# The two halves of a matmul's moving operand read in turn: both products of a dense layer, the spectral mix and the last transform step

## The chip, the cores and the metric

The kernel runs on one core of one Trainium2 chip. The metric is the device time of one launch in microseconds (us), lower is better. Times of before and after are medians over several runs; the profile is one execution, recorded instruction by instruction. PE is TensorE's matmul, PEld its weight load, DVE is VectorE, ACT is ScalarE, SP is SyncE.

## The reference, cut to what matters

A spectral layer is followed by a dense layer with squared ReLU, on 8 sequences of 3008 tokens with 256 features, all float32.

```python
X = np.fft.rfft(x, axis=1)
Yr = Xr @ w_r - Xi @ w_i + b_r
Yi = Xr @ w_i + Xi @ w_r + b_i
Yr = np.sign(Yr) * np.maximum(np.abs(Yr) - 0.01, 0.0)   # Yi likewise
y = np.fft.irfft(Yr + 1j * Yi, n=3008, axis=1)
h = np.maximum(y.reshape(24064, 256) @ w_in, 0.0)       # w_in: 256 x 2048
out = h * h @ w_out                                     # w_out: 2048 x 256
```

## The kernel before, in words

The transform of length 3008 is split in two factors, 47 and 64, and both directions are matmuls with small tables. Stage A is the step over 47, stage B the step over 64, then comes the mix (the product with `w_r` and `w_i`), a threshold, stage C (the inverse step over 64) and stage D (the inverse step over 47). Stages A and C leave their results in DRAM scratch, from which the next stage loads them. The dense layer follows, in 47 chunks of `CH` = 512 tokens; `HALF` is 256.

Most products are made in three matmuls on operands of type float32r: each float32 operand is split in a high and a low part, and `mm3` (lines 183 to 188) issues high x high (L186), high x low (L187) and low x high (L188) into one accumulator. Its first pair of arguments is the stationary operand, of up to 128 columns, which a weight load puts into the array before every matmul; its second pair is the moving operand, whose columns stream through the array and come out in the same order. Stages B and D use plain float32 matmuls (L228, L277), and so does the start's stage A (L488).

After a start of some 130 us, which works on the first two sequences, the kernel runs in rounds. A chunk has `NU` = 8 rounds, and there are 376 rounds and 3 more to finish. Round r does the following on TensorE, in this order:

1. `mm1`: the first product for two blocks of 128 hidden features, 12 matmuls with 512 moving columns each, from the chunk's operand `xt` (tile of 128 x 2 x 512, high and low). In 130 rounds the last of the 12 is made in two halves of 256 columns (L986).
2. at the place called "p1", and again at "p2" behind `mm2`: at each at most one piece of another stage, put there by a planner. Such a piece is stage A (6 matmuls), stage B (8), the mix (18 matmuls of 256 moving columns, with `wm` as the moving operand), stage C (3 of 512 columns, with `zh` and `zl` moving) or stage D (8).
3. `mm2`: the second product for the round three before (`LAG` = 3). It is a fast scheme with 7 block products in place of 8, on 7 combinations `g` of hidden blocks and token halves: 14 matmuls with `gh` (L1023) and 7 with `gl` (L1027), all of 256 moving columns. The last round of all has its own order in `mm2_last` (L1008).

ACT takes `ph` out of PSUM (L995), squares it (L996) and casts the 7 combinations to their high part (L1132); DVE makes the combinations (L1001 to L1003) and the low part (L1137). Behind these stand ACT's and DVE's work for the other stages, among it the copy of stage C's result from PSUM to the tile `evc` (L860), which is stored to scratch. `put_together` (L1030 and after) sums the 7 products of a chunk, and two transfers store it.

The order on every engine is written out by hand: the program issues round after round, place after place, and each engine works strictly in that order. The moving operands are read in rows that lie together: `xt` 512 elements of 4 bytes, `gh`, `gl` and `wm` 256, and `zh`, `zl` 512 over two neighbouring parts `q`.

`tables_main` runs once, at the end of the start, and writes the mix's weights `wm`: the high part by ACT (L180), the low part by DVE (L181), 128 x 768 elements in each of 2 steps. The start's own mix uses the same tile in another layout before that. Also in the start, `narrow` has ACT read every second 4-byte word of a tile of float64 weights (L301), beside casts of the same size that read words in a row (L431).

Of the kernel before, what the change touches and what calls it, by code (L numbers as in the profile page):

```python
# [9 lines left out]
F32 = mybir.dt.float32  # L10
# [6 lines left out]
S = 3008  # L17
# [4 lines left out]
D = 256  # L22
# [112 lines left out]
NU = NF // 2  # L135


CH = 512
HALF = CH // 2


def pair_rounds(nb):
# [9 lines left out]
def fft_mix_moe(ctx: ExitStack, tc: tile.TileContext, xp, xu, w_ri, b_ri,  # L152
                w_in, w_out, t_u, t_a, t_b, t_b0, t_m, t_d, sgn, outT):
    nc = tc.nc
# [6 lines left out]
    def ctile(name, shape, dt=F32):  # L161
        return const.tile(shape, dt, name=name, tag=name)
# [10 lines left out]
    wm = [ctile(f"wm{k}", [P, 3, 2, D], F32R) for k in range(2)]  # L173
    ctile("gap5", [P, 16])
    wi_ = []
    wo_ = [], []

    def split(src, hi, lo, engine=nc.vector):

        nc.scalar.copy(hi, src)  # L180
        engine.tensor_sub(lo, src, hi.bitcast(F32))  # L181
# [18 lines left out]
    def scratch2(b):  # L200
        scr2[b] = dr.tile([NR, N2, 2 * D], F32, tag="s2", name=f"s2_{b}")
# [4 lines left out]
    def load_b(b, i, t):  # L206
        v = scr1[b].rearrange("r n (c d) -> (n c) r d", c=2)
        nc.sync.dma_start(out=t.rearrange("p (q d) -> p q d", q=2), in_=v[:, 2 * i:2 * i + 2, :])
# [22 lines left out]
    def take_b(x, ps):  # L231
        nc.scalar.copy(x[:, 0:2].rearrange("p s k m -> p k s m"),  # L232
                       ps.rearrange("p (k s m) -> p k s m", k=2, s=2))

    def sum_x(x):
        nc.vector.tensor_add(x[:, 2], x[:, 0], x[:, 1])
# [22 lines left out]
    xts = {}  # L259
# [51 lines left out]
    def start():  # L311

        with ExitStack() as own:
# [4 lines left out]
            def tl(tag, shape=(P, 512), dt=F32, bufs=1, name=None):  # L318
                return sb.tile(list(shape), dt, tag=tag, name=name or tag, bufs=bufs)
# [36 lines left out]
            ms = tl("wmf", (P, 6, D))  # L356
# [39 lines left out]
            def tables_main():  # L396

                for k in range(2):
                    split(ms[:, 3 * k:3 * k + 3], wm[0][:, :, k], wm[1][:, :, k])
                    yield  # L400
                split(tM, tMs[:, 0], tMs[:, 1])
                yield
# [102 lines left out]
            xs, pm, zs, pc, got = {}, {}, {}, {}, {}  # L505
# [204 lines left out]
    def tl(tag, shape=(P, 512), dt=F32, bufs=1, name=None):  # L710
        return sb.tile(list(shape), dt, tag=tag, name=name or tag, bufs=bufs)

    def pst(name):
        return ps_f.tile([P, 512], F32, tag="f", name=name)

    def opnd(name, dt, bufs):
        return tl(name, (P, NPR, HALF), dt, bufs=bufs)

    for tag, shape, dt, bufs in (("g", (P, NPR, HALF), F32, 3), ("gh", (P, NPR, HALF), F32R, 2), ("gl", (P, NPR, HALF), F32R, 2),
                                 ("gap1", (P, 16), F32, 1), ("xh", (P, 3, 2, P), F32R, 1), ("xl", (P, 3, 2, P), F32R, 1),  # L720
# [74 lines left out]
    def plan_b(b, i, r):  # L795
        s = {}

        def load():
            if i == 0:
                scratch2(b)  # L800
            s["t"] = tl("ld", bufs=3, name="bin")
            load_b(b, i, s["t"])

        def points():
            s["ps"] = pst("psb")
            points_b(s["ps"], i, s["t"])

        def take():
            s["x"] = tl("x", (P, 3, 2, P), name="x")
            take_b(s["x"], s["ps"])  # L810

        def high():
            s["h"] = tl("xh", (P, 3, 2, P), F32R)
            nc.scalar.copy(s["h"], s["x"])

        def low():
            s["l"] = tl("xl", (P, 3, 2, P), F32R)
            nc.vector.tensor_sub(s["l"], s["x"], s["h"].bitcast(F32))

        def mix():  # L820
            p = s["p"] = pst("psm1"), pst("psm2")
            for comp, mat, bank, half in MIX:
                for k in range(2):
                    mm3(p[bank][:, half * D:half * D + D], (s["h"][:, comp, k], s["l"][:, comp, k]),
                        (wm[0][:, mat, k], wm[1][:, mat, k]), k == 0, k == 1)

        def biased():
            s["et"] = tl("et", (P, 2, 512))
            add_e(s["et"][:, 0], *s["p"])

        def threshold():
            e, t = s["et"][:, 0], s["et"][:, 1]
            nc.vector.tensor_scalar(t, e, LAM, -LAM, op0=ALU.min, op1=ALU.max)
            nc.vector.tensor_sub(e, e, t)

        def turned():
            z = s["z"] = tl("z", (P, 2, D))
            e = s["et"][:, 0].rearrange("p (c e) -> p c e", c=2)
            for q in range(2):
                r = 2 * i + q  # L840
                src = slice(64 * q, 64 * q + 64)
                nc.scalar.copy(z[:64, q], e[src, 0])
                nc.scalar.activation(z[64:, q], e[src, 1], AF.Copy, scale=sg[src, 1, r:r + 1])

        def zhigh():
            s["zh"] = tl("zh", (P, 2, D), F32R)
            nc.scalar.copy(s["zh"], s["z"])

        def zlow():
            s["zl"] = tl("zl", (P, 2, D), F32R)  # L850
            nc.vector.tensor_sub(s["zl"], s["z"], s["zh"].bitcast(F32))

        def back():
            s["ps"] = pst("psc")
            mm3(s["ps"], (tMs[:, 0], tMs[:, 1]),
                tuple(s[k].rearrange("p q e -> p (q e)") for k in ("zh", "zl")), True, True)

        def out():
            e = tl("ev", bufs=2, name="evc")
            nc.scalar.copy(e, s["ps"])  # L860
            store_c(b, i, e)

        at(r - 1, "load", load)
        at(r, "p1", points)
        at(r, "e", take)
        at(r, "e2", lambda: sum_x(s["x"]))
        at(r, "f", high)
        at(r, "v", low)
        at(r + 2, "p2", mix)
        at(r + 2, "f2", biased)  # L870
        at(r + 2, "v", threshold)
        at(r + 3, "a", turned)
        at(r + 4, "a", zhigh)
        at(r + 4, "v", zlow)
        at(r + BACK[b], "p2", back)
        at(r + BACK[b], "f", out)
# [79 lines left out]
    for c in range(1, nch):  # L956
# [5 lines left out]
        for n, part in enumerate(parts):  # L962
            at_b = flat[part[0]][0]
            lo = max(NU * (c - 1), free, rounds[at_b][-1] + BACK[at_b] + 3 if at_b else 2)
            got = spread(len(part), lo, NU * c - 3 - sum(map(len, parts[n + 1:])), D_WORK, 1, BESIDE)
# [5 lines left out]
    def mm1(c, j, halved):  # L971
        if c == 0 and 0 < j < LAG:
            ph = [ps_o.tile([P, CH], F32, tag=f"o{2 * j - 2 + a}", name="ph") for a in range(2)]
        else:
            t = ps_h.tile([P, 2, CH], F32, tag="h", name="ph")
            ph = [t[:, a] for a in range(2)]
        for a in range(2):
            f = 2 * j + a
            fs = slice(f * P, f * P + P)
            for k in range(2):  # L980
                w, x = (wi_[0][:, k, fs], wi_[1][:, k, fs]), (xts[c][0][:, k], xts[c][1][:, k])
                if halved and a and k:
                    nc.tensor.matmul(ph[a], w[0], x[0], start=False, stop=False)  # L983
                    nc.tensor.matmul(ph[a], w[0], x[1], start=False, stop=False)  # L984
                    for n in range(0, CH, HALF):
                        nc.tensor.matmul(ph[a][:, n:n + HALF], w[1], x[0][:, n:n + HALF], start=False, stop=n > 0)  # L986
                else:
                    mm3(ph[a], w, x, k == 0, k == 1)
        return ph
# [15 lines left out]
    def mm2_last(po, gh, gl):  # L1005

        def add(s, bank, half, w, x, stop):
            nc.tensor.matmul(po[bank][:, half * HALF:half * HALF + HALF], w[:, s], x[:, s],  # L1008
                             start=False, stop=stop, skip_group_check=True)

        for n in range(NPR + 2):
            if n < NPR:
                for k in range(2):
                    add(*LAST[n], wo_[k][NU - 1], gh, False)
            if n >= 2:
                add(*LAST[n - 2], wo_[0][NU - 1], gl, True)

    def mm2(j, po, gh, gl):

        for s, bank, half in PLACES:  # L1020
            out = po[bank][:, half * HALF:half * HALF + HALF]
            for k in range(2):
                nc.tensor.matmul(out, wo_[k][j][:, s], gh[:, s], start=j == 0 and half == 0 and k == 0,  # L1023
                                 stop=False, skip_group_check=True)
        for s, bank, half in PLACES:
            out = po[bank][:, half * HALF:half * HALF + HALF]
            nc.tensor.matmul(out, wo_[0][j][:, s], gl[:, s], start=False, stop=j == NU - 1,  # L1027
                             skip_group_check=True)

    def put_together(c, po):  # L1030
# [83 lines left out]
    with tc.manual_schedule():  # L1114
        for r in range(last + LAG):
            c, j = divmod(r, NU)
# [3 lines left out]
            if r < last:  # L1120
                ph = mm1(c, j, (r, "p1") not in plan)
# [3 lines left out]
            k = r - LAG  # L1125
# [86 lines left out]
```

## Time and profile before

| What | Value |
|---|---|
| time, median of 3 runs | 2524.14 us (2523.18 to 2525.43) |
| span of the profiled execution | 2521.5 us |
| TensorE busy with matmuls | 2503.5 us, 99% |
| TensorE busy with weight loads | 2260.2 us, 90% |
| DVE busy | 2097.8 us, 83% |
| ACT busy | 1991.8 us, 79% |
| granted TensorE clock | 1.000, mean of the span |

The span runs from the first to the last instruction of one execution. The page gives no separate time of that execution from outside; the runs' median stands 2.6 us above the span. Matmuls are pipelined, so the busy time of one (0.39 us for 512 columns) is longer than its share of the engine; the distance from one start to the next is that share.

### The profile page before, as it was taken

Reading aid. Unit: us, or ns where it says so; the run is one execution under the profiler, and the core shown is the slowest. Engines: PE = TensorE matmul, PEld = TensorE weight load, DVE = VectorE, ACT = ScalarE, POOL = GpSimd, SP = SyncE. Lnnn points to the kernel's source line nnn. Section 1 sums busy time; section 2 is a strip of 40 time slices with the busy share of each in tenths; the row PEclk is TensorE's granted clock in tenths of the full one; section 3 lists DMA queues with packets and bytes.
Section 4 is the critical chain, followed back from the end, with each engine's and each line's share of the span. In section 5 each row is a group of like instructions: output and inputs, shape, how many; then the busy total and the mean of one; then the engine's idle time right before and its main releaser. Section 6 shows DMA issues by size and latency. Waiting matters only on the chain.

```text
span 2521.5 us, 42247 instructions
## 1 busy us (share of the span) xinstructions
PE 2503.5 (99%) x16648; PEld 2260.2 (90%) x16648; DVE 2097.8 (83%) x3179; ACT 1991.8 (79%) x2776; POOL 17.0 (1%) x29
## 2 busy tenths in 40 slices
PE   9999999999999999999999999999999999999999
PEld 5689999999999999999999999999999999999998
DVE  5798888888888888888888888888887888777776
ACT  4788887888788887888878878788787788777776
POOL 0100000000000000000000000000000000000000
PEclk9999999999999999999999999999999999999999
DMA  8612222222121121212122121221111111101000
GB/s 266 207 55 66 74 88 68 65 76 73 54 75 60 50 70 57 71 50 67 60 69 63 54 70 50 70 62 61 58 56 56 38 54 48 39 21 34 17 25 18
DMA packets 110622, 164.66 MB, mean 65 GB/s; under 512 B 9513, under 2 KB 59673, under 8 KB 110234
## 3 DMA queue, kind: packets, MB, share of 16 engines
q1 hardware_dynamic: 110282, 161.85, 20.9%
q8 instruction: 132, 2.16, 0.4%
q14 instruction: 64, 0.52, 0.1%
q10 hardware_dynamic: 144, 0.13, 0.0%
HBM read 86.97 MB, written 74.97 MB: 64 GB/s over the span
## 4 chain that ended last, share of the span: by engine, by line
PE 88%; ACT 5%; DVE 4%; issue 1%; DMA 1%; SPq 0%; DVEq 0%; ACTq 0%
PE po L1023 21%; PE ph L187 11%; PE ph L188 11%; PE ph L186 11%; PE po L1027 11%; PE psd L277 3%; PE psb L228 3%; PE psm L186 3%; PE psm L188 3%; PE psm L187 3%; ACT g L995 1%; PE ph L986 1%; PE ph L983 1%; PE ph L984 1%; ACT g L996 1%
## 5 line engine op out<-in xcount | busy, mean ns | idle before, releaser
L1137 DVE TENSOR_TENSOR gl<-g,gh 128x1792 fp32r<-128x1792 f32 x376 | 759.5, 2020 | 22.4 <-ACT gh L1132 15.4
L995 ACT ACTIVATE g<-ph 128x512 f32<-128x512 f32 x752 | 408.2, 595 | 417.1 <-PE ph L188 297.4
L1023 PE MATMUL po<-gh,wo 128*128 128x256 f32 x5250 | 681.5, 280 | 3.1 <-DVE o L1053 2.1
L1132 ACT CAST gh<-g 128x1792 fp32r<-128x1792 f32 x376 | 637.2, 1695 | 3.5 <-PE po L1023 0.8
L1023 PEld LDWEIGHTS po<-gh,wo 128*128 128x128 f32 x5250 | 631.2, 188 | 6.5 <-DVE o L1053 5.9
L186 PE MATMUL ph<-xt,wi 128*128 128x512 f32 x1374 | 538.2, 392 | 2.2 <-ACT g L995 2.0
L188 PE MATMUL ph<-xt,wi 128*128 128x512 f32 x1374 | 537.4, 391 | 0.0
L187 PE MATMUL ph<-xt,wi 128*128 128x512 f32 x1374 | 537.3, 391 | 0.0
L1001 DVE TENSOR_TENSOR g<-g 128x512 f32<-128x512 f32 x376 | 259.3, 690 | 290.3 <-ACT g L996 288.4
L996 ACT ACTIVATE g<-g 128x1024 f32<-128x1024 f32 x376 | 399.5, 1062 | 12.0
L1027 PE MATMUL po<-gl,wo 128*128 128x256 f32 x2625 | 359.2, 276 | 0.0
L1027 PEld LDWEIGHTS po<-gl,wo 128*128 128x128 f32 x2625 | 325.7, 188 | 0.0
L188 PEld LDWEIGHTS ph<-xt,wi 128*128 128x128 f32 x1374 | 258.0, 188 | 55.9
L186 PEld LDWEIGHTS ph<-xt,wi 128*128 128x128 f32 x1374 | 257.9, 188 | 49.6 <-ACT g L995 2.8
L187 PEld LDWEIGHTS ph<-xt,wi 128*128 128x128 f32 x1374 | 258.0, 188 | 44.3
L1003 DVE TENSOR_TENSOR g<-g 128x256 f32<-128x256 f32 x376 | 159.9, 425 | 12.9
L1002 DVE TENSOR_TENSOR g<-g 128x256 f32<-128x256 f32 x376 | 159.8, 425 | 12.9
L186 PE MATMUL psm<-wm,xh 128*128 128x256 f32 (+1 forms) x552 | 159.7, 289 | 1.6 <-ACT x L232 1.3
L188 PE MATMUL psm<-wm,xl 128*128 128x256 f32 (+1 forms) x552 | 158.2, 287 | 0.0
L187 PE MATMUL psm<-wm,xh 128*128 128x256 f32 (+1 forms) x552 | 158.0, 286 | 0.0
L277 PEld LDWEIGHTS psd<-tD,din 120*128 120x128 f32 (+1 forms) x832 | 108.2, 191 | 9.7 <-issue 1.9
L228 PEld LDWEIGHTS psb<-tB,bin 128*128 128x128 f32 x768 | 99.8, 191 | 13.1 <-issue 3.7
(139 smaller groups left out, 2800.5 us busy)
## 6 DMA issues: line engine op xcount, KB each, us to landing
bin<-s SPq DMA_DIRECT2D x96, 256.0 KB
s<-evc SPq DMA_DIRECT2D x96, 256.0 KB
outT_dram<-o SPq DMA_DIRECT2D x92, 256.0 KB
din<-s SPq DMA_DIRECT2D x96, 240.0 KB
xin<-in_xp_dram SPq DMA_DIRECT2D x72, 240.0 KB
s<-eva SPq DMA_DIRECT2D x72, 240.0 KB
s<-eva SPq DMA_DIRECT2D x38, 192.0 KB
w<-in_moe_w_in_dram SPq DMA_DIRECT2D x8, 512.0 KB
```

Source lines behind the costliest of these rows:

```text
L186: nc.tensor.matmul(out, l0, r0, start=start, stop=False, **kw)
L187: nc.tensor.matmul(out, l0, r1, start=False, stop=False, **kw)
L188: nc.tensor.matmul(out, l1, r0, start=False, stop=stop, **kw)
L228: nc.tensor.matmul(ps[:, k, :, q, :], tv[:, q, k], tB[:, 0:r + 2:r + 1], start=True, stop=True)
L277: nc.tensor.matmul(ps[:, k, part], t[:n, s:s + P], tD[:n, tab + part, :n], start=True, stop=True)
L995: nc.scalar.activation(g[:, 2 * a:2 * a + 2], ph[a].rearrange("p (t m) -> p t m", t=2), AF.Relu)
L996: nc.scalar.activation(g[:, 0:4], g[:, 0:4], AF.Square)
L1001: nc.vector.tensor_sub(g[:, 4:6], g[:, 1:4:2], g[:, 0:2])
L1023: nc.tensor.matmul(out, wo_[k][j][:, s], gh[:, s], start=j == 0 and half == 0 and k == 0, stop=False, skip_group_check=True)
L1027: nc.tensor.matmul(out, wo_[0][j][:, s], gl[:, s], start=False, stop=j == NU - 1, skip_group_check=True)
L1132: nc.scalar.copy(split_[r - 1][0], hid[r - 1])
L1137: nc.vector.tensor_sub(gl, hid.pop(r - 1), gh.bitcast(F32))
```

## The change

`crossed(x)` takes a view of a moving operand in which its two halves are read in turn: column 0 of the first half, column 0 of the second, column 1 of the first, and so on. In bytes two elements read one after the other lie 1024 apart in `xt`, `zh` and `zl`, and 512 apart in `gh`, `gl` and `wm`. The number of matmuls, their columns and their weights stay as they are. Each product's columns come out in the crossed order, and this is put right at different places:

- `mm1`, `mm2` and `mm2_last`: the columns are tokens, the order stays crossed through both products and the output, and the host puts the tokens in order (`places`).
- the mix: `wm` is stored crossed by `tables_main`, so that reading it crossed gives its columns in order.
- stage C: its columns come out crossed in PSUM, and ACT's copy to `evc` reads them in a row and writes them in turn to the two halves of the tile.

Stages A, B and D and the start are as before.

```diff
+def crossed(x):
+    return x.rearrange("p (a i) -> p i a", a=2)
+
+def places(n):
+    return np.arange(n).reshape(2, n // 2).T.reshape(-1)
...
                 for k in range(2):
-                    split(ms[:, 3 * k:3 * k + 3], wm[0][:, :, k], wm[1][:, :, k])
+                    hi, lo = (wm[h][:, :, k].rearrange("p m (a i) -> p m i a", a=2) for h in range(2))
+                    src = ms[:, 3 * k:3 * k + 3].rearrange("p m (i a) -> p m i a", a=2)
+                    nc.scalar.copy(hi, src)
+                    nc.vector.tensor_sub(lo, src, hi.bitcast(F32))
...
                     mm3(p[bank][:, half * D:half * D + D], (s["h"][:, comp, k], s["l"][:, comp, k]),
-                        (wm[0][:, mat, k], wm[1][:, mat, k]), k == 0, k == 1)
+                        (crossed(wm[0][:, mat, k]), crossed(wm[1][:, mat, k])), k == 0, k == 1)
...
             mm3(s["ps"], (tMs[:, 0], tMs[:, 1]),
-                tuple(s[k].rearrange("p q e -> p (q e)") for k in ("zh", "zl")), True, True)
+                tuple(s[k].rearrange("p q e -> p e q") for k in ("zh", "zl")), True, True)
...
-            nc.scalar.copy(e, s["ps"])
+            nc.scalar.copy(e.rearrange("p (q e) -> p e q", q=2), s["ps"].rearrange("p (e q) -> p e q", q=2))
...
-                w, x = (wi_[0][:, k, fs], wi_[1][:, k, fs]), (xts[c][0][:, k], xts[c][1][:, k])
+                w, x = (wi_[0][:, k, fs], wi_[1][:, k, fs]), (crossed(xts[c][0][:, k]), crossed(xts[c][1][:, k]))
...
-                        nc.tensor.matmul(ph[a][:, n:n + HALF], w[1], x[0][:, n:n + HALF], start=False, stop=n > 0)
+                        nc.tensor.matmul(ph[a][:, n:n + HALF], w[1], x[0][:, n // 2:(n + HALF) // 2], start=False, stop=n > 0)
...
-            nc.tensor.matmul(po[bank][:, half * HALF:half * HALF + HALF], w[:, s], x[:, s],
+            nc.tensor.matmul(po[bank][:, half * HALF:half * HALF + HALF], w[:, s], crossed(x[:, s]),
...
-                nc.tensor.matmul(out, wo_[k][j][:, s], gh[:, s], start=j == 0 and half == 0 and k == 0,
+                nc.tensor.matmul(out, wo_[k][j][:, s], crossed(gh[:, s]), start=j == 0 and half == 0 and k == 0,
...
-            nc.tensor.matmul(out, wo_[0][j][:, s], gl[:, s], start=False, stop=j == NU - 1,
+            nc.tensor.matmul(out, wo_[0][j][:, s], crossed(gl[:, s]), start=False, stop=j == NU - 1,
```

## Rows read from the trace of the kernel before

**Rows 1.** The page's busy times (us, share, instructions) and granted clock by slice.

```profile
PE 2503.5 (99%) x16648; PEld 2260.2 (90%) x16648; DVE 2097.8 (83%) x3179; ACT 1991.8 (79%) x2776; POOL 17.0 (1%) x29
...
PEclk9999999999999999999999999999999999999999
```

**Rows 2.** TensorE's own waits, longest first: total us, times, longest.

```profile
PE psa L488 <- DMA x<-in_xu_dram: 2.3, 2, 1.2
PE po L1023 <- DVE o L1053: 2.1, 11, 0.3
PE ph L186 <- ACT g L995: 2.0, 2, 1.6
```

**Rows 3.** The page's chain that ended last, shares of the span by engine.

```profile
PE 88%; ACT 5%; DVE 4%; issue 1%; DMA 1%; SPq 0%; DVEq 0%; ACTq 0%
```

**Rows 4.** PE's timeline, first product of one round, 9 matmuls apart: start us, us.

```profile
1211.96 0.39 PE L186 MATMUL ph<-xt,wi 128*128 128x512 f32 x1
...
1214.00 0.28 PE L186 MATMUL psa<-fh,tAs 120*120 120x256 f32 x1
```

**Rows 5.** PE's timeline, the mix of another round, 15 matmuls apart.

```profile
301.20 0.28 PE L188 MATMUL psm<-wm,xl 128*128 128x256 f32 x1
...
302.90 0.28 PE L188 MATMUL psm<-wm,xl 128*128 128x256 f32 x1
```

**Rows 6.** PE's timeline in the start: 16 plain float32 matmuls in a row.

```profile
13.47 7.03 PE L488 MATMUL psa<-x,tU 96*96 96x512 f32 x16
```

**Rows 7.** PEld's timeline, a stage B piece: 7 weight loads in a row.

```profile
1201.23 0.86 PEld L228 LDWEIGHTS psb<-tB,bin 128*128 128x128 f32 x7
```

**Rows 8.** Groups by line and shape: count | busy us, mean ns | idle before.

```profile
L1023 PE MATMUL po<-gh,wo 128*128 128x256 f32 x5250 | 681.5, 280 | 3.1 <-DVE o L1053 2.1 <-DVE o L1036 0.3
L186 PE MATMUL ph<-xt,wi 128*128 128x512 f32 x1374 | 538.2, 392 | 2.2 <-ACT g L995 2.0
L1027 PE MATMUL po<-gl,wo 128*128 128x256 f32 x2625 | 359.2, 276 | 0.0
L186 PE MATMUL psm<-wm,xh 128*128 128x256 f32 x504 | 139.5, 277 | 1.3 <-ACT x L232 1.3
L228 PEld LDWEIGHTS psb<-tB,bin 128*128 128x128 f32 x768 | 99.8, 191 | 13.1 <-issue 3.7 <-PE psm L188 1.4 <-DVE et L242 0.4
L986 PE MATMUL ph<-xt,wi 128*128 128x256 f32 x260 | 51.5, 280 | 0.0
L983 PE MATMUL ph<-xt,wi 128*128 128x512 f32 x130 | 50.6, 389 | 0.0
L860 ACT COPY evc<-psc 128x512 f32<-128x512 f32 x84 | 49.1, 584 | 0.0
L186 PE MATMUL psc<-zh,tMs 128*128 128x512 f32 x84 | 33.4, 397 | 0.0
L488 PE MATMUL psa<-x,tU 96*96 96x512 f32 x64 | 28.8, 595 | 2.3 <-DMA x<-in_xu_dram 2.3
L301 ACT ACTIVATE w<-w 128x512 f32<-128x512 f32 x13 | 8.7, 669 | 5.2 <-DMA w<-in_moe_w_in_dram 5.2
L431 ACT CAST wi<-w 128x512 fp32r<-128x512 f32 x8 | 5.0, 621 | 0.2
L1008 PE MATMUL po<-gh,wo 128*128 128x256 f32 x14 | 2.3, 276 | 0.0
L1008 PE MATMUL po<-gl,wo 128*128 128x256 f32 x7 | 1.7, 291 | 0.0
L181 DVE TENSOR_TENSOR wm<-wmf,wm 128x768 fp32r<-128x768 f32 x2 | 1.8, 954 | 0.0
L180 ACT CAST wm<-wmf 128x768 fp32r<-128x768 f32 x2 | 1.6, 830 | 0.0
```

**Rows 9.** Windows: stretch, length, busy us (count) by engine, clock, DMA, GB/s.

```profile
500.00:1000.00 500.00, 499.75 (x3410) 459.32 (x3409) 428.51 (x656) 408.14 (x575) 0.00 (x0) 1.00 0.21 64
1018.80:1032.60 13.80, 13.69 (x97) 12.54 (x96) 11.42 (x22) 13.46 (x21) 0.00 (x0) 1.00 0.14 38
```

More of the change, by code (lines that the diff above doesn't have):

```diff
@@ L1206 @@
     got = np.asarray(r.results[0]["outT_dram"])
-    got = got.reshape(D, nb, S)
+    chunks = np.empty((D, nb * S // CH, CH), got.dtype)
+    chunks[:, :, places(CH).reshape(2, HALF)[:, places(HALF)].reshape(-1)] = got.reshape(D, -1, CH)
+    got = chunks.reshape(D, nb, S)
     out = np.empty((nb, S, D), got.dtype)
```

## The prediction

> **What bounds the kernel now.** [...] Then TensorE's own waits: the longest total is 2.3 us, and the three longest together make 6.4 us [rows 2]. No other engine holds TensorE up, and what sets the end is the time that its matmuls take to stream. The chain of work agrees: 88% of it runs through TensorE, 5% through ACT and 4% through DVE [rows 3]. The last two shares matter later: they are stretches in which TensorE is busy, but only just.
>
> "Busy" doesn't say whether the matmuls run as fast as they could, so I took the distance from one start to the next. In a run of the first product, 9 matmuls of 512 columns lie within 1214.00 - 1211.96 = 2.04 us, 226.7 ns each [rows 4]. In the mix, 15 matmuls of 256 columns lie within 302.90 - 301.20 = 1.70 us, 113.3 ns each [rows 5]. [...]
>
> [...]
>
> **The change part by part.**
>
> Nothing is removed or added on TensorE: the same matmuls, columns and weight loads. The only thing that changes there is the order in which moving columns are read. The crossed matmuls are 3 x 1374 + 2 x 130 = 4382 of the first product and 3 x 84 = 252 of stage C with 512 columns, 4634 together; and 5250 + 2625 + 14 + 7 = 7896 of the second product, 3 x 504 = 1512 of the mix and 260 half matmuls of the first product with 256 columns, 9668 together [rows 8]. [...]
>
> How a crossed read costs isn't shown by any row: no moving operand here is read in turns. The bounds:
>
> [...]
> [...]
> - Loss by the nearest row: ACT reading every second word took 669 ns (L301), and a cast of 512 words in a row 621 ns (L431), 8% more [rows 8]. The functions differ, so it is a rough row. [...]
> [...]
>
> [...]
>
> - **512 columns**: 213.3 + 2.3 = 215.6 ns in place of 226.7, 11.1 ns x 4634 = 51.4 us.
> - **256 columns**: 106.7 + 2.3 = 109.0 by the stream, but each matmul needs a weight load of 128 columns. Seven of these in a row took 0.86 us [rows 7]; less the last one's 0.19 (L228) [rows 8] that is 0.67 / 6 = 112 ns each. I take 112 as the floor: 113.3 - 112 = 1.3 ns x 9668 = 12.6 us. If loads can come faster, it is 4.3 ns, 41.6 us.
>
> Together 64 us. Two things are taken off:
>
> - **What is late next.** Where the chain runs through ACT or DVE, 9% of the span [rows 3], a faster TensorE only waits longer. One such stretch, at the end of a chunk, has ACT busy for 13.46 of 13.80 us, while a long window has it at 82% and DVE at 86% [rows 9]. I take off 9% of 64, 6 us.
> - **ACT's copy of stage C** writes to two places in turn. 84 copies of 584 ns (L860) [rows 8]: by the 8% above +4 us on ACT, if a write in turns takes double, +49 us. It lies beside TensorE's work except where ACT is the chain (5%), so 0.2 to 2.5 us; I take 1. If that cover went, all of the +49 would count.
>
> The new order of `wm` in the start is 2 casts of 830 ns and 2 subtractions of 954 ns (L180 and L181) [rows 8]; doubled they are 3.6 us more, beside the weights' other work, and I cost them at nothing. No transfer changes in size or place, no wait is added, and the host's ordering isn't in the metric. PSUM is written in a row as before.
>
> Sum: 64 - 6 - 1 = 57 us. The profiled span of 2521.5 becomes 2464.5; the runs' median lies 2.6 us over the span, so 2467 us.
>
> [...]
>
> **The rivals.**
>
> [...]
>
> [...]
>
> [...]
>
> **How the numbers follow.** A measurement of this kernel can tell some 0.2%, 5 us, from no change. I give the faster case 0.62 (2395 to 2505, likeliest 2467): the loss per 64 bytes is the one thing in these rows that an order of reading could act on. Nothing happens: 0.18 (2519 to 2529). Slower: 0.20, of which half rate 0.13 and a milder loss 0.07. The range holds the first two cases, 0.80, and goes from 2395 to 2535 with room for slower copies. Its upper end stops short of the slower cases; the likeliest case's own range is 2395 to 2505.
>
> **What would show it.** Right: starts of the first product 215 to 217 ns apart in place of 226.7, of the second product and the mix 109 to 112 in place of 113.3; stage A's, which stay in a row, as before; idle time on TensorE rising to some microseconds behind ACT at chunk ends; L860 longer than 584 ns. Wrong: starts 227 ns apart (nothing happens) or near 427 (half rate). The forecast also fails if the distance falls but TensorE then waits for ACT or DVE in every round, which the waits would show as tens of microseconds.

## The result

The changed kernel takes 2484.14 us (median of 4 runs, 2483.76 to 2484.53) against 2523.66 us: a ratio of 0.9844, 95% interval 0.983 to 0.9858, 39.5 us less. The forecast was 2467 us. Medians here and below are over fast runs: one execution of the kernel before without ACT's squaring took 13361 us and is left out.

The page of the changed kernel, its span and the busy times (us, share, instructions), to be read against [rows 1]:

```profile
span 2482.1 us, 42239 instructions
...
PE 2443.1 (98%) x16648; PEld 2244.5 (90%) x16648; DVE 2094.8 (84%) x3179; ACT 2026.8 (82%) x2776; POOL 17.1 (1%) x29
```

TensorE's busy time fell by 60.4 us, the span by 39.4. The difference is idle time: 39 us where there were 18. ACT is busy for 35 us more, although it has the same instructions.

PE's timeline of the changed kernel, first product of one round and the mix of another (start us, us), the counterparts of [rows 4, 5]:

```profile
1211.74 0.38 PE L196 MATMUL ph<-xt,wi 128*128 128x512 f32 x1
...
1213.90 0.38 PE L997 MATMUL ph<-xt,wi 128*128 128x512 f32 x1
```

```profile
301.09 0.28 PE L196 MATMUL psm<-wm,xh 128*128 128x256 f32 x1
...
302.76 0.28 PE L196 MATMUL psm<-wm,xh 128*128 128x256 f32 x1
```

The first two are 10 matmuls apart, 2.16 us: 216 ns each, where it was 226.7. The other two are 15 apart, 1.67 us: 111 ns, where it was 113.3. Both distances are those of the forecast (215.6 and 112). In the second product the median distance is 112 ns, where it was 113.

What the forecast had only as its far end, a write in turns that takes double, stands in the groups by line and shape (count | busy us, mean ns | idle before), to be read against L860, L180 and L181 of [rows 8]:

```profile
L873 ACT COPY evc<-psc 128x512 f32<-128x512 f32 x84 | 92.1, 1097 | 0.0
...
L412 DVE TENSOR_TENSOR wm<-wmf,wm 128x768 fp32r<-128x768 f32 x2 | 3.2, 1718 | 0.8 <-ACT wm L411 0.8
L411 ACT CAST wm<-wmf 128x768 fp32r<-128x768 f32 x2 | 3.1, 1670 | 0.0
```

Writing in turn to two halves took ACT 1097 ns in place of 584, and about doubled the two steps of `wm` as well (that of DVE also reads the high part in turn). TensorE's own waits (total us, times, longest), against [rows 2]:

```profile
PE ph L196 <- ACT g L1008: 9.3, 15, 2.1
PE po L1036 <- DVE o L1066: 4.8, 16, 0.3
PE psb L238 <- DVE et L252: 3.5, 10, 0.6
PE po L1036 <- ACT xt L299: 2.8, 5, 0.7
PE psm L196 <- ACT x L242: 2.6, 5, 1.6
```

None of these five was over 2.1 us before. How such a wait comes about is seen in a stretch of the timeline of all engines:

```profile
227.22 1.06 ACT L1009 ACTIVATE g<-g 128x1024 f32<-128x1024 f32 x1
...
228.18 0.57 ACT L242 COPY x<-psb 128x512 f32<-128x512 f32 x1
...
228.80 0.38 PE L196 MATMUL psm<-wm,xh 128*128 128x256 f32 x1 [0.33 <-ACT x L242]
```

The mix fills two PSUM buffers, `psm1` and `psm2`, out of a pool of two for all stages. The second still holds stage B's result, which ACT copies out (L242), but only behind the squaring (L1009). The mix stops after its first six matmuls until that copy is done. The chain of work of the changed kernel breaks off at the program's end in this profile and isn't used.

### The profile page after: what moved, and what is told of

It reads as the page before. It is cut to its first block, busy times and chain, and to the rows that moved or that the text cites. A ratio compares the mean times of both kernels' runs of the same rounds, so it can differ in the third digit from the quotient of the medians.

```text
span 2482.1 us, 42239 instructions
## 1 busy us (share of the span) xinstructions
PE 2443.1 (98%) x16648; PEld 2244.5 (90%) x16648; DVE 2094.8 (84%) x3179; ACT 2026.8 (82%) x2776; POOL 17.1 (1%) x29
## 3 DMA queue, kind: packets, MB, share of 16 engines
q8 instruction: 132, 2.16, 0.4%
## 5 line engine op out<-in xcount | busy, mean ns | idle before, releaser
L1036 PE MATMUL po<-gh,wo 128*128 128x256 f32 x5250 | 667.5, 278 | 8.4 <-DVE o L1066 4.8
L1036 PEld LDWEIGHTS po<-gh,wo 128*128 128x128 f32 x5250 | 618.0, 192 | 13.4 <-DVE o L1066 8.0
L196 PE MATMUL ph<-xt,wi 128*128 128x512 f32 x1374 | 525.8, 383 | 9.8 <-ACT g L1008 9.3
L197 PE MATMUL ph<-xt,wi 128*128 128x512 f32 x1374 | 521.6, 380 | 0.0
L198 PE MATMUL ph<-xt,wi 128*128 128x512 f32 x1374 | 521.4, 379 | 0.0
L1009 ACT ACTIVATE g<-g 128x1024 f32<-128x1024 f32 x376 | 400.0, 1064 | 11.9
L196 PEld LDWEIGHTS psm<-wm,xh 128*128 128x128 f32 x552 | 105.6, 191 | 12.8 <-ACT x L242 4.7
```

The costliest lines, as they stand in the source:

```text
L196: nc.tensor.matmul(out, l0, r0, start=start, stop=False, **kw)
L197: nc.tensor.matmul(out, l0, r1, start=False, stop=False, **kw)
L198: nc.tensor.matmul(out, l1, r0, start=False, stop=stop, **kw)
L1009: nc.scalar.activation(g[:, 0:4], g[:, 0:4], AF.Square)
L1036: nc.tensor.matmul(out, wo_[k][j][:, s], crossed(gh[:, s]), start=j == 0 and half == 0 and k == 0, stop=False, skip_group_check=True)
```

## The experiments

Each kernel is the changed one but for the edit, unless it says otherwise. Times are medians; a ratio is against the kernel before, measured beside it (2523.67 to 2524.34 us).

### What ACT's slow copy costs: two ways to be rid of it

First, stage C put back as it was:

```diff
-                tuple(s[k].rearrange("p q e -> p e q") for k in ("zh", "zl")), True, True)
+                tuple(s[k].rearrange("p q e -> p (q e)") for k in ("zh", "zl")), True, True)
...
-            nc.scalar.copy(e.rearrange("p (q e) -> p e q", q=2), s["ps"].rearrange("p (e q) -> p e q", q=2))
+            nc.scalar.copy(e, s["ps"])
```

> The changed kernel with stage C alone put back: its 252 matmuls read zh and zl in a row and ACT's copy writes in a row. Theory A (the doubled copies, 84 x 0.51 us on ACT, make TensorE wait for PSUM banks and for ACT's later work): the 252 matmuls lose 2.8 us, TensorE's new idle time of some 20 us mostly goes, the median falls from 2484 to 2463 to 2472 us. Theory B (a faster TensorE meets ACT and DVE at their limit anyway, the copies matter little): only the 2.8 us are lost, 2485 to 2489 us.

Second, the same copy with its order turned round: SBUF is written in a row, PSUM is read at every second word.

```diff
-            nc.scalar.copy(e.rearrange("p (q e) -> p e q", q=2), s["ps"].rearrange("p (e q) -> p e q", q=2))
+            nc.scalar.copy(e.rearrange("p (q e) -> p q e", q=2), s["ps"].rearrange("p (e q) -> p q e", q=2))
```

> The changed kernel, but ACT's copy of stage C reads every second word of PSUM and writes SBUF in a row. Theory A, if it is the write in turns that doubles the copy: copies at some 590 ns, TensorE's new waits mostly gone, 2460 to 2469 us, some 3 us better than with stage C put back. Theory A, if any access out of a row doubles it: copies near 1100 ns and 2484 us as before. Theory B: 2481 to 2485 us whatever the copies take.

Measured: 2469.29 us (ratio 0.9782, 0.9768 to 0.9795) and 2466.32 us (0.9772, 0.9758 to 0.9785). Both intervals lie clear below that of the change. In the second kernel the copies are back at their length, while its products all read in turn:

```profile
L873 ACT COPY evc<-psc 128x512 f32<-128x512 f32 x84 | 49.1, 585 | 0.0
```

So it is the write out of a row that doubles the copy (1097 ns); reading PSUM out of a row costs nothing here, 585 ns where the copy in a row took 584. Theory A holds, and theory B falls as the whole account: 17.8 us of the gain went into a copy that ACT makes 84 times. The 2.97 us between the two kernels agree with the 2.8 that stage C's matmuls should bring, but their intervals overlap.

### Is it ACT's time, or the write itself?

The kernel of 2466 us with each copy made twice, both writing in a row:

```diff
             nc.scalar.copy(e.rearrange("p (q e) -> p q e", q=2), s["ps"].rearrange("p (e q) -> p q e", q=2))
+            nc.scalar.copy(e.rearrange("p (q e) -> p q e", q=2), s["ps"].rearrange("p (e q) -> p q e", q=2))
```

> As the run whose copy reads PSUM out of a row (2466 us), but each of the 84 copies of stage C is made twice, one after the other, into the same tile. ACT has then 0.585 us more per copy, 49 us in all, and no write is out of a row. Theory A (what costs is ACT's time, in the place where the copy stands): back to 2482 to 2490 us, as with the slow copy (2484). Rival D (the write in turns itself disturbs TensorE's reads or the store to scratch): 2466 to 2471 us.

And the kernel before, moving operands in a row, with the slow copy alone:

```diff
-            nc.scalar.copy(e, s["ps"])
+            nc.scalar.copy(e.rearrange("p (q e) -> p e q", q=2), s["ps"].rearrange("p (e q) -> p e q", q=2))
```

> The kernel before, all moving operands in a row, with the slow copy alone: stage C's columns are written in turn to the two halves, so that the inverse step gets them in another order and the output is another one. [...] Theory A without cover (the copy costs its 18 us at any pace of TensorE): 2538 to 2545 us.

Measured: 2496.70 us (0.9891, 0.9878 to 0.9905) and 2534.72 us (1.0042, 1.0028 to 1.0056). Time of ACT alone, with no write out of a row, costs as much and more: 30.4 us for 49 us of ACT, 6.7 over theory A's window. Rival D's 2466 to 2471 us did not come, and it falls as the explanation; why 49 us of a second copy cost more than the 17.8 of the longer one wasn't settled. In the kernel before the copy is as slow:

```profile
L860 ACT COPY evc<-psc 128x512 f32<-128x512 f32 x84 | 93.2, 1110 | 0.0
```

It costs 10.7 us there (7 to 14 by the interval), less than the 18 of theory A without cover: of its 43 us (84 x 0.51) 32 didn't show in the time at TensorE's old pace, 227 ns for 512 columns, and 25 at the new one, 216 ns. So it is likely that cover went with TensorE's pace, but it was not whole at the old one either.

### What the new order is worth with ACT at leisure

Two kernels without ACT's squaring, that of 2466 us and the kernel before:

```diff
-        nc.scalar.activation(g[:, 0:4], g[:, 0:4], AF.Square)
```

> As the run whose copy reads PSUM out of a row (2466 us), but ACT's squaring of the hidden layer is left out (376 instructions of 1.06 us, 400 us of ACT; the output is that of a layer without the square). Theory N (the gain still missing there, some 20 us between the matmuls' faster steps and the time, is TensorE waiting for a chain through ACT): 2440 to 2450 us. Rival V (it waits for DVE, whose work stays): 2460 to 2466 us.

> The kernel before without ACT's squaring (the output is that of a layer without the square), the control of the run before. TensorE hardly waits there, so both theories expect little: 2512 to 2524 us. The distance to the run before is then what the new reading order is worth with ACT at leisure: some 75 us by theory N, 55 to 60 us by rival V.

Measured: 2436.43 us (0.9653, 0.964 to 0.9666) and 2510.99 us (0.9949, 0.9934 to 0.9965). The first is 3.6 us under the window of theory N, far from rival V's, the second 1.0 under its own. With ACT at leisure the new order is worth 74.6 us; with the squaring and the quick copy it was 2524.34 - 2466.32 = 58.0. So another 16.5 us, some 6 either way by the intervals, go to waits for ACT's chain which TensorE's old pace hid. Without the squaring, 1.06 us long (L996), DVE also gets its input about that much earlier in each round, so this is the chain through ACT, not ACT's busy time alone. The windows of a long stretch (busy us and count of PE, PEld, DVE, ACT, POOL, then clock, DMA share, GB/s) show it, that of the quick copy first, then without the squaring:

```profile
500.00:1000.00 500.00, 498.38 (x3505) 468.26 (x3504) 437.55 (x667) 416.21 (x584) 0.00 (x0) 1.00 0.22 66
```

```profile
500.00:1000.00 500.00, 499.92 (x3537) 472.72 (x3536) 442.23 (x678) 345.17 (x516) 0.00 (x0) 1.00 0.21 65
```

TensorE gets through 3537 matmuls in place of 3505 with ACT at 69% in place of 83%, and DVE at 88% doesn't hold it up. In [rows 9] it was 3410. The same 500 us don't hold quite the same pieces, so these counts support the times and don't replace them.

### The first product alone

Second product, mix and stage C as in the kernel before; a part of the edit:

```diff
-                nc.tensor.matmul(out, wo_[k][j][:, s], crossed(gh[:, s]), start=j == 0 and half == 0 and k == 0,
+                nc.tensor.matmul(out, wo_[k][j][:, s], gh[:, s], start=j == 0 and half == 0 and k == 0,
...
-                        (crossed(wm[0][:, mat, k]), crossed(wm[1][:, mat, k])), k == 0, k == 1)
+                        (wm[0][:, mat, k], wm[1][:, mat, k]), k == 0, k == 1)
```

> Only the first product reads its halves in turn; second product, mix and stage C read in a row, ACT's copies as in the kernel before. By the forecast's sum the 512-column matmuls of the first product bring 4382 x 11.1 = 48.6 us, less some 4 us of new waits: 2523.7 to 2479 us. Theory A says the same, since no copy is longer: 2475 to 2482. Theory B (a faster TensorE waits anyway): the waits take 15 to 20 of the 48.6 us, 2490 to 2495 us.

Measured: 2486.97 us (0.9853, 0.9839 to 0.9866), 37.4 us less than before, between the two windows; it decides nothing between A and B. Its first product gained what it should: the median over the rounds from its first start to that of the next piece fell from 2743 to 2589 ns. But the second product, whose matmuls are as before, got longer, from 2465 to 2494 ns in the mean, 11 us over 372 rounds; its median rose by 7 ns, and the length that one in ten exceeds rose from 2485 to 2557. Why just there wasn't settled. The step from this kernel to the one with stage C put back, 17.7 us, is what the second product and the mix bring.

### Which orders help

The first product in another order in each chunk of 512 tokens, eleven orders by turns:

```diff
+ORDERS = [
+    lambda x: x,
+    crossed,
+    lambda x: x.rearrange("p (a i) -> p i a", a=4),
+    lambda x: x.rearrange("p (i a) -> p a i", a=2),
+    lambda x: x.rearrange("p (a i j) -> p i a j", a=2, j=2),
+    lambda x: x.rearrange("p (a i j) -> p i a j", a=2, j=16),
+] + [lambda x, n=n: x.rearrange("p (b a i) -> p b i a", a=2, i=n) for n in (2, 4, 8, 16, 32)]
```

> The changed kernel, in which the first product reads its 512 moving columns in another order in each chunk, eleven orders by turns, never in two halves; the output's tokens stay in these orders, they are not put right. What counts is the distance between two starts of the first product by order, in steady stretches. In a row 226.7 ns, halves in turn 215.7 ns by the runs so far. Theory L (one clock is lost when the stream goes on to the next 64 bytes, and it is hidden if another line is read in between): runs of 16 columns from the two halves in turn stay near 227, groups of 2, 4 or 8 columns swapped within 64 bytes stay near 227, blocks of 16 or 32 columns in turn and quarters in turn go to 216, every second column (8 bytes apart) near 240. Rival W (a clock is lost by reading neighbouring words in successive clocks, so that any order which breaks the row helps): 216 for all orders but the row and the runs of 16. Rival F (the trait is one of far distance, such as different banks): only halves, pairs from the halves and quarters reach 216, all the blocks stay at 227 or get slower.

A second kernel of this kind took `"p (i a) -> p a i"` with a=4 (every fourth word), `"p (a i t) -> p t i a"` (every second word of two halves in turn) and `"p (b a i) -> p b i a"` with a=4, i=4 (four stretches of 16 bytes in turn).

> The first product reads its columns in another order in each chunk, five orders by turns; the output's tokens stay in these orders. In a row 227 ns and halves in turn 216 as before. [...] Four lines of 16 bytes next to each other in turn: 283 ns like the quarters, if the distance doesn't matter.

PE's timeline, 5 matmuls apart each: three chunks of the first kernel (blocks of four words in turn, groups of 2 swapped, every second word) and one of the second (every fourth word):

```profile
521.77 0.38 PE L206 MATMUL ph<-xt,wi 128*128 128x512 f32 x1
...
522.85 0.38 PE L208 MATMUL ph<-xt,wi 128*128 128x512 f32 x1
```

```profile
480.38 0.39 PE L206 MATMUL ph<-xt,wi 128*128 128x512 f32 x1
...
481.51 0.40 PE L208 MATMUL ph<-xt,wi 128*128 128x512 f32 x1
```

```profile
287.60 0.64 PE L206 MATMUL ph<-xt,wi 128*128 128x512 f32 x1
...
289.86 0.63 PE L208 MATMUL ph<-xt,wi 128*128 128x512 f32 x1
```

```profile
227.69 0.64 PE L205 MATMUL ph<-xt,wi 128*128 128x512 f32 x1
...
229.99 0.64 PE L207 MATMUL ph<-xt,wi 128*128 128x512 f32 x1
```

1.08 / 5 = 216 ns, 1.13 / 5 = 226, 2.26 / 5 = 452 and 2.30 / 5 = 460. The kernels took 2645.30 and 2735.70 us, one execution each; their times aren't used, since every chunk differs. All orders, each the median over 192 or more matmuls (the 6th to 11th of every run of twelve):

| Order of the 512 columns | ns | ns a column |
|---|---|---|
| in a row | 227 | 0.443 |
| groups of 2 swapped, inside 16 bytes | 227 | 0.443 |
| blocks of 4, 8, 16 or 32 words in turn (16 to 128 bytes apart) | 216 | 0.422 |
| halves in turn (1024 bytes apart) | 216 | 0.422 |
| every second word of two halves in turn | 227 | 0.443 |
| runs of 16 words from two halves in turn | 240 | 0.469 |
| four stretches of 16 bytes in turn | 268 | 0.523 |
| quarters in turn | 283 | 0.553 |
| pairs of words from two halves in turn | 333 | 0.650 |
| every second word | 452 | 0.883 |
| every fourth word | 461 | 0.900 |

Theory L falls: blocks of 4 and 8 words change nothing in how often 64 bytes are passed, and they help in full (216 ns). Rival W falls with the groups of 2 (227 ns), rival F with the blocks of 4 (216 ns). What the orders at 216 ns share, and no other of the table has, is this: the words come one by one in turn from two stretches of 16 bytes, and both are read to their end before the next two. Two neighbouring stretches of 8 bytes in turn, the groups of 2, took 227 ns like the row. Every fourth word, one out of each 16 bytes, took 461 ns, hardly more than the 452 of every second word, two out of each.

### A better version

The kernel of 2466 us with stage A read in turn too, its copy reading PSUM out of a row:

```diff
-                    (s["h"][:, cs], s["l"][:, cs]), True, True)
+                    (crossed(s["h"][:, cs]), crossed(s["l"][:, cs])), True, True)
...
-            nc.scalar.copy(e, s["o"])
+            nc.scalar.copy(e.rearrange("p (c a i) -> p c a i", c=2, a=2), s["o"].rearrange("p (c i a) -> p c a i", c=2, a=2))
```

> As the run whose copy reads PSUM out of a row (2466 us), with stage A's 480 or so matmuls of 256 columns reading their halves in turn as well, and ACT's copy of stage A reading every second word of PSUM. If the reading order helps there as elsewhere, a stage A matmul goes from some 117 ns to 109 to 112: 2.4 to 3.8 us less and no longer copy, 2462 to 2465 us. Rival: these pieces are set by ACT and DVE around them: 2465 to 2469 us.

Measured: 2463.68 us (0.976, 0.9747 to 0.9774), the fastest of the kernels that compute the whole layer, 60.0 us under the kernel before. Stage A's high x low matmuls went from a median of 118 to 109 ns apart, with its copies at 573 ns. The step from 2466.32 is what was forecast, but the two intervals overlap, so it is likely and not shown.

## Why the forecast was right, and where its terms were off

**Bound.** That TensorE's streaming sets the time, and that the order of reading acts on it, held: the order alone moved the distance from 227 to 216 ns in the first product and from 113 to 111 in the mix.

**The 64 bytes.** Why the order helps was not as forecast. The forecast tied the loss to every 64 bytes, which was the author's estimate; theory L is that idea, and it fell. Blocks of 4 words in turn, which pass from one 64 bytes to the next no less often than the row, took 216 ns, so two stretches of 16 bytes in turn are enough. The trace of before, in which all these operands are read in a row (226.7 and 113.3 ns), couldn't tell 64 bytes from 16. Two far halves in turn satisfy both readings, so the choice of the order came out right by luck in this respect.

**The streams, 64 us forecast.** No run shows the 213.3, 106.7 and 2.3 ns that this sum starts from; the runs showed distances of 216 ns for 512 columns, and of 111 and 112 for 256. Measured by the median length of each kind of run, 81 us: the first product 2743 to 2592 ns (151 ns x 372 rounds = 56 us), the second 2473 to 2425 (18 us), stage C 706 to 650 and the mix 2040 to 2010 (84 of each, 7 us). With ACT at leisure 74.6 us came out as time. The term was too small because it went by the steady distance. In the round of [rows 4] the first matmuls of the run were further apart:

```profile
1211.26 0.39 PE L186 MATMUL ph<-xt,wi 128*128 128x512 f32 x1
```

To the start at 1211.96, three matmuls later, these are 233 ns each, and that surplus went with the new order as well: in the changed kernel the median distance is 218 ns for the first and 216 from the second on. The step from the last matmul to the next piece fell too, from 235 to 216 ns in the median. The matmuls of 256 columns came to 111 ns in the mix and 112 in the second product, close to the 112 ns of a weight load in [rows 7], as forecast; stage A, with loads of 120 columns, came to 109 in the last experiment. That the loads are the floor is still an estimate: no run changed them alone.

**What is late next, 6 us forecast.** Of the gross 81 us, 42 didn't arrive. Without the slow copy it is still 24 (less the copy's 17.8), four times the term; 16.5 of that go to ACT's chain by the kernels without the squaring, and the remaining 7 aren't laid to anything. Taking the chain's 9% for ACT and DVE as the share that is lost was the error: the chain names the stretches that were at the limit at the old pace, not those that come to it at the new one. Waits of tens of microseconds were also the forecast's own sign of failing. Idle time did rise by 21 us, but not in every round: the longest group above is 15 waits in 376 rounds.

**The copy, 1 us forecast, 0.2 to 2.5.** Measured 17.8 us. Two things were mis-sized. The length, by a row of ACT reading every second word (8%), where writing in turn took 88% more (1097 ns against 584); the upper end, double, was the true one. And its share on the path, 5% by the chain, where 41% of the 43 us came through. The truth lies between the range's upper end of 2.5 and the sentence that all of the 49 would count if the cover went.

Two errors partly cancelled, and that is luck: the streams gained 17 us more than forecast, and the waits and the copy took 35 us more. That leaves 39.5 us of gain where 57 were forecast.

**The rivals.** Half rate did not come (216 ns, not near 427), and "nothing happens" is out. Nor did the time come near the range's lower end of 2395 us, which no run bears out: with ACT at leisure the new order was worth 74.6 us, and that kernel took 2436. A slower stream is out for the crossed order as well: two stretches of 16 bytes read in turn took 216 ns, less than four successive words of each, 227. Other orders did slow it: every fourth word took 461 ns. In the table, what a column costs goes with how many stretches are read in turn (216 ns for two, 268 for four of 16 bytes) and how much of each is taken (227 ns for every second word of two halves), and the trace of before had no row for it.

## What to carry to other kernels

Where float32r matmuls read their moving operand in a row, here 227 ns apart for 512 columns, try an order in which successive columns come from two stretches of 16 bytes in turn, here 216 ns, and put the columns in order where it costs little: on the host, in weights stored once (some 3 us on ACT and DVE here), or in a copy that reads PSUM out of a row and writes SBUF in a row (585 ns here, as long as before). When the engine at 99% is made faster, price what the others do at its new pace: ACT, at 80% on average, took some 34 of the 81 us that the streams gave, 17.8 by its slow copy and 16.5 by its chain. Before an order is spread over four places, take the cost of undoing it from a run of its own.

## What the runs showed of the hardware that was not expected

- A matmul of 512 columns took 227 ns with its columns in a row, 216 with two stretches of 16 bytes in turn, 268 to 283 with four in turn, and 333 with pairs of words from two halves.
- If every 16 bytes that the stream passes cost the same, which by the row is 4 x 227 / 512 = 1.77 ns (an estimate), every second word would take 454 ns and every fourth 908. Every second word took 452, every fourth 461. So this doesn't hold as a rule, and what lies behind the table stays open.
- ACT's copy of 128 x 512 from PSUM took 585 ns when it read every second word there, as long as in a row (584), and 1097 ns when it wrote in turn to two halves of SBUF.
